# Queries' transposes ahead of the weights' fetches, and a new home for four weights, in an attention and MLP kernel

## The chip, the cores and the metric

The kernel runs on one core of a Trainium2 chip. The metric is the device time of one execution in microseconds. Its engines are named as in the profile: PE multiplies matrices (PEld loads its weights), DVE is the vector engine, ACT the scalar engine, POOL the GpSimd engine, and SP issues nearly all DMA transfers, in the order of its queue.

## What is computed

Attention over clusters, and a two-layer MLP on its result. For 4 batches and 8 heads, 768 queries and keys of 64 elements are each assigned to one of 16 clusters; a query sees only the keys of its own cluster.

```python
q_assign = argmax(q_n @ c_n.T)
k_assign = argmax(k_n @ c_n.T)
scores = scale * q @ k.T
scores = where(q_assign == k_assign, scores, -1e9)
attn = softmax(scores)
x = (attn @ v), heads joined: 3072 tokens x 512
r = maximum(x @ w_in, 0.0)
g = s * (r * r) + b
out = g @ w_out
```

w_in is 512x2048 and w_out 2048x512. All inputs and outputs are f32; the argmax and the result are computed with each f32 number as a sum of two f16 numbers, a high and a low part.

## The kernel before, in words

**Units and steps.** The attention is cut into 192 units: batch b, a third of the query rows c (256 rows), a head pair hp, one of two row tiles t, and a head h. A unit is a score product (scores, L491, into PSUM), its row maximum on DVE (maxima, L501), a bias and an exponential on ACT (exps, L508 and L511), a transposition of the result, and the product with the values. The MLP has 192 steps too: 12 blocks of 256 rows by 16 slices ft of the hidden layer. A step is a product h (mlp_in, L647), a ReLU and two squares on ACT (mlp_relu, L654 to L657), a low part on POOL (mlp_gl, L662) and the second product acc (mlp_out, L674). The main loop goes over i: unit i, the values of unit i-4, and MLP step i-21 (`LAG`).

**The first 16 units** (`RAW`) differ: the exponentials are transposed in f32 on PE (low, L535) and copied out of PSUM by DVE and ACT (L137, L135), and two units at a time are multiplied by the f32 values (values, L557, bank "m" of PSUM) and scaled on DVE (L574). After four units finish_x multiplies by the scale of the values (ACT L607), makes the high part xn (ACT L611), takes an absolute maximum (DVE L114), makes the low part (POOL L614) and transposes by DMA. After four of these, DVE L622 and a PE product find the largest x of the block, and mlp_start (L632 to L638) makes the factor that the first ReLU needs.

**Before unit 0.** prep_k and prep_q load keys and queries, scale them by a power of two, split them into high and low parts (ka, qa) and transpose these by DMA (KA, L357; QA, L411). PE multiplies KA and QA by the transposed centroids cT (pk, L366; pq, L420; cT's own transpose is L176), and onehot (L308 to L314) turns the scores into masks kb and qb, which are transposed too (KB, L370; QB, L424). A unit's scores are QA by KA plus QB by KB.

**The weights.** 32 pieces of 512 KB are fetched (fetch, through three staging buffers "stage" or gs), decoded (rebase on ACT L225; narrow on DVE L229 and L230) and bounded (bound: ACT L237 or L239, PE L242, DVE L243). The last piece lets finish_w_in and finish_w_out (DVE L264 to L279) make the two global factors; with them wsplit (ACT L287, DVE L289; 32 of each) cuts every piece into high and low parts for the MLP. The pieces and their split parts share 33 buffers of tag "w", one more than there are pieces, so each split writes into the buffer that the split before has emptied.

**What sets the order.** A scheduler places each engine's instructions by a simulated timeline and by priorities: `first_of_all` raises the priority of units under 20. `behind(x)` puts an instruction after x on the same engine's queue; it adds no wait on the hardware. The order ahead of the loop is written out at the end of the function (L740 to L768), as here:

```python
    with behind(last_turn[0], *last_split):
        some(first_v, 1)
...
        some(wgen, 4)
```

## Time and profile before

| what | value |
|---|---|
| median of three runs | 925.96 us (924.53 to 930.2) |
| the profiled execution's own time | 923.07 us |
| its span, first to last instruction | 921.4 us |
| PE busy | 829.3 us, 90% of the span |
| DVE, ACT, POOL busy | 638.4, 712.3, 545.8 us |
| mean granted clock of PE | 0.962 of full speed |

Shares of busy time are means over stages with different limits. There is a head, in which PE has little to do while keys, queries and weights are made ready; a middle, in which the first units, the splits of the weights and the first MLP steps overlap; and a long steady part with one unit and one MLP step per round. In the rows, "x" ahead of a number counts instructions, and what stands in brackets at a row's end is the idle time of that engine just before, with what ended it. The time of an execution is 1.67 us longer than its span.

### The profile page before, as it was taken

To read this page: it belongs to the slowest core of one execution; us is meant where nothing else is said; L and a number is where in the kernel's file an instruction comes from. 1 tells how busy PE (TensorE), PEld (TensorE's weight loads), DVE (VectorE), ACT (ScalarE), POOL (GpSimd) and SP (SyncE) were. 2 spreads that over 40 slices of the span, in tenths; PEclk is the share of its full clock that TensorE was granted. 3 is DMA by queue.
4 is the path that set the end of the run, shared out by engine and by line. 5 is a ranking of instruction groups with operands and counts; after the bars stand their busy time and mean duration, and the time that the engine had idled before them with its cause. 6 is when DMAs were issued, how large, how long until landed. Compare 5 with 4: busy or idle time off the path is not lost.

```text
span 921.4 us, 22828 instructions
## 1 busy us (share of the span) xinstructions
PE 829.3 (90%) x8625; PEld 589.0 (64%) x8625; DVE 638.4 (69%) x1672; ACT 712.3 (77%) x1408; POOL 545.8 (59%) x580
## 2 busy tenths in 40 slices
PE   0566877797999999999999989999999999999997
PEld 0345765564566767777667757776677777677764
DVE  7699779999676768756976567669868557563200
ACT  3479867676678879889888878988888789788553
POOL 3011127565667767777778558667776667676322
PEclk9987587998999999999999999999999999999999
DMA  6898815874786997997999888789998777666300
GB/s 174 208 276 256 223 41 104 194 155 104 172 156 143 201 189 149 170 184 143 183 181 169 182 167 164 165 166 184 177 158 169 147 133 163 121 140 142 64 24 23
DMA packets 437758, 144.23 MB, mean 157 GB/s; under 512 B 405392, under 2 KB 434064, under 8 KB 437648
## 3 DMA queue, kind: packets, MB, share of 16 engines
q1 hardware_dynamic: 437648, 142.78, 74.5%
q8 instruction: 67, 1.10, 0.5%
q14 instruction: 43, 0.35, 0.2%
HBM read 35.69 MB, written 6.29 MB: 46 GB/s over the span
## 4 chain that ended last, share of the span: by engine, by line
PE 50%; DVE 15%; DMA 8%; ACT 5%; issue 4%; POOL 2%; SPq 1%; DVEq 0%; ACTq 0%; POOLq 0%
PE h L647 18%; PE acc L674 17%; PE sc L491 7%; DMA kn<-in_k_dram 3%; DVE ssm L501 3%; DMA qn<-in_q_dram 2%; PE sc L589 2%; PE sc L591 2%; PE sc L590 2%; DVE wos L289 1%; DMA vn<-in_v_dram 1%; DVE wis L289 1%; ACT ssm L508 1%; DMA QB<-qb 1%; SPq L545 1%
## 5 line engine op out<-in xcount | busy, mean ns | idle before, releaser
L543 POOL TENSOR_TENSOR ph<-p,ph 128x768 f16<-128x768 f32 x176 | 296.8, 1687 | 148.5 <-ACT ph L135 50.0
L647 PE MATMUL h<-xk,wis 128*128 128x256 f16 x2304 | 289.1, 275 | 10.0 <-DVE wis L289 4.5
L674 PE MATMUL acc<-wos,gs 128*128 128x512 f16 x1152 | 281.7, 380 | 5.2 <-POOL gs L662 3.8
L647 PEld LDWEIGHTS <-wis 128*128 128x128 f16 x2304 | 223.0, 98 | 68.8 <-issue 7.1
L511 ACT ACTIVATE p<-sc,ssm,qsm 128x768 f32<-128x768 f32 x192 | 189.3, 986 | 4.1
L501 DVE TENSOR_REDUCE ssm<-sc 128x1 f32<-128x768 f32 x192 | 181.9, 948 | 4.1 <-PE sc L491 3.8
L662 POOL TENSOR_TENSOR gs<-r,gs 128x256 f16<-128x256 f32 x192 | 138.5, 722 | 70.6 <-ACT r L657 62.1
L674 PEld LDWEIGHTS <-gs 128*128 128x128 f16 x1152 | 104.2, 98 | 100.4 <-POOL gs L662 5.0
L508 ACT ACTIVATE ssm<-ssm,lift,qsm 128x1 f32<-128x1 f32 x192 | 73.1, 381 | 92.0 <-DVE ssm L501 90.8
L135 ACT ACTIVATE ph<-p 128x768 f16<-128x768 f32 x164 | 137.2, 837 | 0.4
L654 ACT ACTIVATE r<-h,cf 128x256 f32<-128x256 f32 x192 | 89.1, 465 | 35.5 <-PE h L647 31.1
L491 PE MATMUL sc<-KA,QA 128*128 128x384 f16 x384 | 98.6, 338 | 18.0 <-ACT p L511 13.8
L589 PE MATMUL sc<-vh,PT 128*128 128x65 f16 x1032 | 112.6, 195 | 1.1 <-DMA PT<-ph 1.1
L590 PE MATMUL sc<-vl,PT 128*128 128x64 f16 x1032 | 112.6, 192 | 0.0
L591 PE MATMUL sc<-vh,PT 128*128 128x65 f16 x1032 | 112.3, 193 | 0.0
L589 PEld LDWEIGHTS <-PT 128*128 128x128 f16 x1056 | 98.7, 97 | 12.8 <-DMA PT<-ph 1.9
L491 PE MATMUL sc<-KB,QB 128*128 128x384 f16 x384 | 99.3, 339 | 7.3 <-DMA QB<-qb 7.3
L590 PEld LDWEIGHTS <-PT 128*128 128x128 f16 x1056 | 97.9, 99 | 11.5 <-issue 0.5
L591 PEld LDWEIGHTS <-PT 128*128 128x128 f16 x1056 | 98.1, 97 | 0.0
L657 ACT ACTIVATE r<-r 128x256 f32<-128x256 f32 x192 | 79.2, 413 | 3.9
L595 DVE TENSOR_SCALAR ssm<-sc 128x1 f32<-128x1 f32 x172 | 26.3, 153 | 80.5 <-PE sc L591 79.3
L656 ACT ACTIVATE gs<-r 128x256 f16<-128x256 f32 x192 | 78.7, 411 | 1.4
(170 smaller groups left out, 1107.5 us busy)
## 6 DMA issues: line engine op xcount, KB each, us to landing
wst<-in_moe_w_in_dram SPq DMA_DIRECT2D x16, 512.0 KB, 4.7
kn<-in_k_dram SPq DMA_DIRECT2D x16, 384.0 KB, 4.0
qn<-in_q_dram SPq DMA_DIRECT2D x24, 256.0 KB, 3.6
vn<-in_v_dram SPq DMA_DIRECT2D x16, 384.0 KB, 4.0
out_dram<-o SPq DMA_DIRECT2D x12, 512.0 KB, 3.3
wst<-in_moe_w_out_dram SPq DMA_DIRECT2D x8, 512.0 KB, 4.8
gs<-in_moe_w_out_dram SPq DMA_DIRECT2D x8, 512.0 KB, 5.4
PT<-ph SPq DMA_TRANSPOSE x176, 3.5
```

Source lines behind the costliest of these rows:

```text
L135: A.activation(dst, src, AF.Copy)
L491: last_score[0] = nc.tensor.matmul(sc[:, e, :HALF], X[:, col, :], y[:, h * S + e * HALF : h * S + (e + 1) * HALF], start=st, stop=not st)
L501: last_max[0] = V.tensor_reduce(SM[i // 4][:, 0, j : j + 1], U[i]["sc"], axis=AX.XY, op=ALU.max, negate=True)
L511: last_exp[0] = A.activation(p.rearrange("p (a b) -> p a b", a=2), u["sc"], AF.Exp, bias=bi, scale=u["scale"], **total)
L543: G.tensor_tensor(u["ph"][:, 1, :], u["p"], u["ph"][:, 0, :], op=ALU.subtract)
L589: nc.tensor.matmul(o1, PT[:, kt, :], vh[:, h, kt, : D + 1], start=(kt == 0), stop=False)
L590: nc.tensor.matmul(o, PT[:, kt, :], vl[:, h, kt, :], start=False, stop=False)
L591: nc.tensor.matmul(o1, PT[:, T + kt, :], vh[:, h, kt, : D + 1], start=False, stop=(kt == T - 1))
L647: nc.tensor.matmul(ph[:, :CW], WSP[ft][0][:, wl, kt, :], XS[(b, c, kt)][:, :, xl, :], start=(i == 0), stop=(i == len(terms) - 1))
L654: A.activation(r, ph[:, :CW], AF.Relu, scale=MS[(b, c)][0])
L662: G.tensor_tensor(g[:, 1, :], r, g[:, 0, :], op=ALU.subtract)
L674: nc.tensor.matmul(acc[:, t, :], g[:, gl, rows], WSP[ft][1][:, wl, :], start=(ft == 0 and gl + wl == 0), stop=(ft == NF - 1 and gl == 1))
```

## The change

- **Order of the head.** The queries are taken one stage further ahead of the weights. The first two fetches of weights and the two scalars sv and bv now stand behind the transposes of the first queries and of the centroids (`last_qa`, `last_c`); the first piece of v, the next two fetches and the decoding of the first weight stand behind the transpose of the queries' mask and the mask itself (`last_qb`, `last_mask`).
- **Four weights live elsewhere.** Three pieces (10, 11 and 12) lie in the fifth buffer of the transposed keys, and one (31) in the fifth buffer of the split values, until they are split. So the 33 buffers of tag "w" hold 28 pieces, and five are free when the splits begin. To allow it, keys and values get fixed storage, `keys` and `halves`; batch 1's first values are split no earlier than step 36.
- **Splits from ft 4 on** stand behind xn and the absolute maximum of the fourth finish_x.
- **Values come a step earlier** (at even i for i-4, before at odd i for i-5), the fourth finish_x runs at once, and for units 8 to 15 the scale of the values is folded into the reciprocal, so that two of the four L607 go.
- **The second third's queries** (b 0, c 1) use bank "h" of PSUM for their maximum and cluster scores, not "m".

```diff
@@ -46,6 +46,7 @@
     URGENT = 20
+    SCALED = 8
 
@@ -173,7 +178,7 @@
     cT = const([P, 3, P], F16, "cT")
-    nc.sync.dma_start_transpose(cT, cnat.rearrange("p a e d -> p (a e d)"))
+    last_c = nc.sync.dma_start_transpose(cT, cnat.rearrange("p a e d -> p (a e d)"))
 
@@ -183,6 +188,20 @@
     xs_kept = const([P, 9, CT, 2, P], F16, "xk")
+
+    keys = const([P, 5, 2, 2 * T * P], F16, "keys")
+    VHW = 2 * T * (D + 2)
+    VLW = 2 * T * D
+    halves = const([P, 5, VHW + VLW], F16, "halves")
+    TW = 2 * KT * P
+    lent = {31: halves[:, 4, :TW]}
+    for j in range(3):
+        lent[10 + j] = keys[:, 4].rearrange("p e x -> p (e x)")[:, j * TW : (j + 1) * TW]
+
+    def raw_tile(p, name):
+        if p in lent:
+            return lent[p].bitcast(F32).rearrange("p (a f) -> p a f", a=KT)
+        return weight_tile(name)
 
@@ -208,10 +227,10 @@
         if p % 2 == 0:
-            w = wi[ft] = weight_tile(f"wi{ft}")
+            w = wi[ft] = raw_tile(p, f"wi{ft}")
             src = w_in.bitcast(I32)[:, ft * 2 * P : (ft + 1) * 2 * P].rearrange("(t p) f -> p t f", p=P)
         else:
-            w = wo[ft] = weight_tile(f"wo{ft}")
+            w = wo[ft] = raw_tile(p, f"wo{ft}")
             src = w_out.bitcast(I32)[ft * P : (ft + 1) * P, :].rearrange("p (a f) -> p a f", a=KT)
@@ -284,9 +303,11 @@
             e = parts(weight_tile(f"w{'io'[len(made)]}s{ft}"))
-            A.activation(e[:, 0], w, AF.Copy, scale=f)
+            with behind(*first_x[: 2 * (ft >= 4)]):
+                A.activation(e[:, 0], w, AF.Copy, scale=f)
             yield
-            V.scalar_tensor_tensor(e[:, 1], w, f, e[:, 0], op0=ALU.mult, op1=ALU.subtract)
+            with behind(*first_x[: 2 * (ft >= 4)]):
+                V.scalar_tensor_tensor(e[:, 1], w, f, e[:, 0], op0=ALU.mult, op1=ALU.subtract)
             made.append(e)
@@ -311,7 +332,7 @@
         V.tensor_tensor(o, e, m.unsqueeze(2).broadcast_to([P, nb, C]), op=ALU.is_equal)
-        eng.tensor_scalar(dst, o.unsqueeze(2).broadcast_to([P, nb, 4, C]), mul, add, op0=ALU.mult, op1=ALU.add)
+        last_mask[0] = eng.tensor_scalar(dst, o.unsqueeze(2).broadcast_to([P, nb, 4, C]), mul, add, op0=ALU.mult, op1=ALU.add)
 
@@ -351,8 +372,7 @@
         G.tensor_copy(kb[:, :, :, 0, :], ka[:, :, :, 0, :])
-        KA = sb.tile([P, 2 * T, P], F16, tag="KA", name=f"KA_{n}", bufs=5)
-        KB = sb.tile([P, 2 * T, P], F16, tag="KB", name=f"KB_{n}", bufs=5)
+        KA, KB = (keys[:, (b * NP + hp) % 5, e].rearrange("p (n q) -> p n q", q=P) for e in range(2))
         KS[(b, hp)] = (KA, KB)
@@ -387,7 +407,7 @@
             yield
-        allmax(sm[:, 1, :], qm, f"q{n}", "m" if b or c else "h")
+        allmax(sm[:, 1, :], qm, f"q{n}", "m" if b or c > 1 else "h")
         yield
@@ -408,10 +428,10 @@
         QS[(b, c, hq)] = (QA, QB, sm)
-        nc.sync.dma_start_transpose(QA, qa.rearrange("p h t e d -> p (h t e d)"))
-        yield
-        yield
-        pa = small_bank(f"pq_{n}", "m" if b or c else "h")
+        last_qa[0] = nc.sync.dma_start_transpose(QA, qa.rearrange("p h t e d -> p (h t e d)"))
+        yield
+        yield
+        pa = small_bank(f"pq_{n}", "m" if b or c > 1 else "h")
         for h in range(nh):
@@ -454,12 +474,17 @@
         V.tensor_scalar(vm[:, 7:8], vm[:, 7:8], 2.0 ** 13, None, op0=ALU.mult)
+        if b == 0:
+            V.tensor_scalar(vm[:, 4:5], vm[:, 6:7], 2.0 ** -13, None, op0=ALU.mult)
         V.tensor_scalar(vm[:, 6:7], vm[:, 6:7], 2.0 ** -19, None, op0=ALU.mult)
...
                 yield from until(RAW - 2 + 2 * hp)
-            vh = sb.tile([P, 2, T, D + 2], F16, tag="vh", name=f"vh_{b}_{hp}", bufs=5)
-            vl = sb.tile([P, 2, T, D], F16, tag="vl", name=f"vl_{b}_{hp}", bufs=5)
+            if b == 1 and hp == 0:
+                yield from until(LAG + NF - 1)
+            both = halves[:, (b * NP + hp) % 5]
+            vh = both[:, :VHW].rearrange("p (h t d) -> p h t d", h=2, t=T)
+            vl = both[:, VHW:].rearrange("p (h t d) -> p h t d", h=2, t=T)
             VS[(b, hp)] = (vh, vl)
@@ -567,7 +592,10 @@
         sums = SM[g][:, 2, j : j + 2] if i < RAW else pu[:, :, D]
-        V.tensor_scalar(rl, sums, 1e-9 * 2.0 ** 14, None, op0=ALU.add)
+        if SCALED <= i < RAW:
+            V.tensor_scalar(rl, sums, 1e-9 * 2.0 ** 14, VM[0][:, 4:5], op0=ALU.add, op1=ALU.mult)
+        else:
+            V.tensor_scalar(rl, sums, 1e-9 * 2.0 ** 14, None, op0=ALU.add)
         V.reciprocal(rl, rl)
@@ -603,13 +631,14 @@
         xs = XT.pop(g)
-        if 4 * g < RAW:
+        if 4 * g < min(SCALED, RAW):
             A.activation(xs, xs, AF.Copy, scale=VM[0][:, 7:8])
...
         xn = sb.tile([P, CT, 2, 2, D], F16, tag="xn", name=f"xn_{g}", bufs=1)
-        A.activation(xn[:, :, 0], xs, AF.Copy)
-        absmax(XM[(b, c)][:, hp : hp + 1], xs.rearrange("p t h d -> p (t h d)"))
+        made = [A.activation(xn[:, :, 0], xs, AF.Copy), absmax(XM[(b, c)][:, hp : hp + 1], xs.rearrange("p t h d -> p (t h d)"))]
+        if g == NP - 1:
+            first_x[:] = made
         yield
@@ -753,17 +782,20 @@
     some(first_k[1], 1)
+    some(first_q[0], 1)
     with behind(*last_split):
...
                 next(gen)
-    with behind(last_turn[0], *last_split):
-        some(first_v, 1)
+    with behind(last_qa[0], last_c, *last_split):
+        some(wgen, 2)
         sv = scalar_in(s_in, "sv")
         bv = scalar_in(b_in, "bv")
-        some(wgen, 4)
     run(first_k[0])
     run(first_q[0])
+    with behind(last_qb[0], last_mask[0]):
+        some(first_v, 1)
+        some(wgen, 2)
     run(first_k[1])
@@ -801,11 +833,13 @@
             mlp_gl(*steps[m - 1])
-        if i >= 5 and i % 2 == 1 and i - 5 < TURN:
+        if i >= 4 and i % 2 == 0 and i - 4 < TURN:
             with first_of_all(i):
-                values(i - 5)
-            if (i - 5) % 4 == 2:
-                active.append(finish_x((i - 5) // 4))
+                values(i - 4)
+                if i - 4 == TURN - 2:
+                    run(finish_x((i - 4) // 4))
+                elif (i - 4) % 4 == 2:
+                    active.append(finish_x((i - 4) // 4))
         background()
```

**SP's queue behind the first keys' transpose, before.** The names after the arrow tell the source: vn is v, wst and gs are staging of weights.

```order
L357 DMA_TRANSPOSE KA_1_204<-ka_170 128x12x128
L83 DMA vn_0_249<-in_v_dram 128x2x384
L141 DMA sv<-in_moe_s_dram 128x1
L141 DMA bv<-in_moe_b_dram 128x1
L83 DMA wst_256<-in_moe_w_in_dram 128x4x256
L176 DMA_TRANSPOSE cT<-cnat 128x3x128
L83 DMA wst_259<-in_moe_w_out_dram 128x1024
L83 DMA wst_262<-in_moe_w_in_dram 128x4x256
L83 DMA gs<-in_moe_w_out_dram 128x1024
L411 DMA_TRANSPOSE QA_0_0_199<-qa_0_0_185 128x8x128
L370 DMA_TRANSPOSE KB_0_194<-kb 128x12x128
L424 DMA_TRANSPOSE QB_0_0_200<-qb_0_0_186 128x8x128
```

The same place with the change:

```order
L377 DMA_TRANSPOSE keys<-ka_172 128x12x128
L181 DMA_TRANSPOSE cT<-cnat 128x3x128
L431 DMA_TRANSPOSE QA_0_0_199<-qa_0_0_187 128x8x128
L88 DMA wst_247<-in_moe_w_in_dram 128x4x256
L88 DMA wst_250<-in_moe_w_out_dram 128x1024
L146 DMA sv<-in_moe_s_dram 128x1
L146 DMA bv<-in_moe_b_dram 128x1
L390 DMA_TRANSPOSE keys<-kb 128x12x128
L444 DMA_TRANSPOSE QB_0_0_200<-qb_0_0_188 128x8x128
L88 DMA vn_0_319<-in_v_dram 128x2x384
L88 DMA wst_322<-in_moe_w_in_dram 128x4x256
L88 DMA gs<-in_moe_w_out_dram 128x1024
```

cT moves up past v, the scalars and one weight, QA past v, the scalars and four weights, KB and QB past v and two weights.

**DVE from the first keys' mask to the queries' mask, before** (oo and oe are steps of onehot, kb and qb the masks, wi and wo weights in decoding):

```order
L314 TENSOR_SCALAR kb<-oo_k_0_296 128x12x64
L230 SCALAR_TENSOR_TENSOR wi_261<-wst_262,wi_261 128x512
L229 TENSOR_SCALAR wo_267<-wo_267 128x512
L230 SCALAR_TENSOR_TENSOR wo_267<-gs,wo_267 128x512
L308 TENSOR_REDUCE om_q_0_0_321<-pq_0_0_304 128x8
L309 TENSOR_TENSOR oe_q_0_0_322<-pq_0_0_304,om_q_0_0_321 128x128
L311 TENSOR_TENSOR oe_q_0_0_322<-oe_q_0_0_322,rev 128x128
L312 TENSOR_REDUCE om_q_0_0_321<-oe_q_0_0_322 128x8
L313 TENSOR_TENSOR oo_q_0_0_323<-oe_q_0_0_322,om_q_0_0_321 128x128
L308 TENSOR_REDUCE om_k_1_356<-pk_1_331 128x12
L314 TENSOR_SCALAR qb_0_0_186<-oo_q_0_0_323 128x8x64
```

With the change, L248 and L249 are the old L229 and L230, and L329 to L335 the old L308 to L314:

```order
L335 TENSOR_SCALAR kb<-oo_k_0_283 128x12x64
L329 TENSOR_REDUCE om_q_0_0_308<-pq_0_0_291 128x8
L330 TENSOR_TENSOR oe_q_0_0_309<-pq_0_0_291,om_q_0_0_308 128x128
L332 TENSOR_TENSOR oe_q_0_0_309<-oe_q_0_0_309,rev 128x128
L333 TENSOR_REDUCE om_q_0_0_308<-oe_q_0_0_309 128x8
L334 TENSOR_TENSOR oo_q_0_0_310<-oe_q_0_0_309,om_q_0_0_308 128x128
L329 TENSOR_REDUCE om_k_1_354<-pk_1_329 128x12
L335 TENSOR_SCALAR qb_0_0_188<-oo_q_0_0_310 128x8x64
L248 TENSOR_SCALAR wi_246<-wi_246 128x512
L248 TENSOR_SCALAR wo_249<-wo_249 128x512
L330 TENSOR_TENSOR oe_k_1_355<-pk_1_329,om_k_1_354 128x192
L249 SCALAR_TENSOR_TENSOR wi_246<-wst_247,wi_246 128x512
```

Four weights' decoding stood among the masks of keys and queries; now none stands ahead of the queries' mask qb, and two follow it.

**ACT from the fourth high part xn to the first ReLU, before** (wis and wos are split parts):

```order
L287 ACTIVATE wis_1524<-wi_480,glob 128x512
L611 ACTIVATE xn_1448<-xs_1366 128x2x128
L287 ACTIVATE wos_1594<-wo_488,glob 128x512
L511 ACTIVATE p_1419<-sc_1410,ssm_1313,qsm_1_0_822 128x768
L508 ACTIVATE ssm_1480<-ssm_1480,lift,qsm_1_0_822 128x1
L287 ACTIVATE wis_1596<-wi_548,glob 128x512
L654 ACTIVATE r_0_0_1579<-h_0_0_1566,cf_0_1562 128x256
L287 ACTIVATE wos_1653<-wo_556,glob 128x512
L656 ACTIVATE gs<-r_0_0_1579 128x256
L657 ACTIVATE r_0_0_1579<-r_0_0_1579 128x256
```

With the change (L307 is the old L287, L639 the old L611, L536 and L533 the old L511 and L508, L683 the old L654), the beginning of it:

```order
L639 ACTIVATE xn_1397<-xs_1332 128x2x128
L307 ACTIVATE wis_1577<-wi_542,glob 128x512
L307 ACTIVATE wos_1634<-wo_550,glob 128x512
L307 ACTIVATE wis_1640<-keys,glob 128x512
L307 ACTIVATE wos_1700<-keys,glob 128x512
L307 ACTIVATE wis_1705<-keys,glob 128x512
L307 ACTIVATE wos_1781<-wo_684,glob 128x512
L307 ACTIVATE wis_1785<-wi_722,glob 128x512
L536 ACTIVATE p_1428<-sc_1419,ssm_1303,qsm_1_0_819 128x768
L533 ACTIVATE ssm_1469<-ssm_1469,lift,qsm_1_0_819 128x1
L307 ACTIVATE wos_1863<-wo_730,glob 128x512
L307 ACTIVATE wis_1865<-wi_790,glob 128x512
```

Ahead of the first ReLU stood two splits after xn; now fifteen stand there, these nine and six more, with three exponentials, two biases and one copy ph among them.

## Rows read from the trace of the kernel before

**Rows 1.** Busy time of each engine in stretches of the span (window: length, then busy us and instructions of PE, PEld, DVE, ACT and POOL; then PE's granted clock, the DMA engines' share and GB/s).

```profile
0.00:36.00 36.00, 6.24 (x82) 3.90 (x83) 27.82 (x91) 14.53 (x26) 10.58 (x42) 1.00 0.67 179
36.00:120.00 84.00, 62.78 (x437) 48.27 (x435) 71.26 (x172) 66.22 (x144) 9.90 (x12) 0.76 0.86 235
145.00:260.00 115.00, 97.85 (x998) 65.42 (x998) 101.34 (x224) 83.95 (x161) 72.41 (x66) 0.94 0.72 149
260.00:866.00 606.00, 593.26 (x6643) 423.59 (x6641) 413.17 (x1122) 508.49 (x997) 430.48 (x433) 1.00 0.83 162
```

**Rows 2.** SP's queue in the order of time: start, length, what is issued.

```profile
15.26 0.59 SPq L83 DMA_DIRECT2D vn<-in_v_dram  x1
...
17.54 1.19 SPq L176 DMA_TRANSPOSE cT<-cnat  x1
...
22.19 1.43 SPq L411 DMA_TRANSPOSE QA<-qa  x1
...
32.84 1.23 SPq L424 DMA_TRANSPOSE QB<-qb  x1
...
41.11 1.25 SPq L86 DMA_DIRECT2D wst<-in_moe_w_in_dram  x1
```

**Rows 3.** What PE waited for up to 140 us (total us, times, longest), and, from the view of transfers between 10 and 45 us, how many of a kind were issued and the median us from issue to landing.

```profile
PE pk L366 <- DMA cT<-cnat: 6.2, 1, 6.2
...
PE sc L491 <- DMA QA<-qa: 4.1, 1, 4.1
...
KA<-ka SPq DMA_TRANSPOSE x4, 3.6
...
cT<-cnat SPq DMA_TRANSPOSE x1, 6.3
...
QB<-qb SPq DMA_TRANSPOSE x1, 2.8
```

**Rows 4.** POOL's copy that completes qa, and DVE from the last keys' split to the first row maximum, in the order of time.

```profile
19.05 0.61 POOL L407 COPY qa<-qb 128x512 f16<-128x512 f16 x1
...
21.85 1.01 DVE L206 SCALAR_TENSOR_TENSOR ka<-kn,ksm,ka 128x768 f16<-128x768 f32 x1
...
24.66 0.36 DVE L308 TENSOR_REDUCE om_k<-pk 128x12 f32<-128x192 f32 x1 [1.53 <-PE pk L367]
...
32.49 0.28 DVE L314 TENSOR_SCALAR qb<-oo_q 128x512 f16<-128x512 f16 x1
...
34.40 0.36 DVE L314 TENSOR_SCALAR xk<-oo_k 128x768 f16<-128x768 f16 x1
...
36.52 1.82 DVE L501 TENSOR_REDUCE ssm<-sc 128x1 f32<-128x768 f32 x2 [1.77 <-PE sc L491]
```

**Rows 5.** Stretches as in Rows 1, shorter.

```profile
36.00:46.60 10.60, 7.96 (x61) 5.45 (x59) 5.66 (x9) 5.25 (x12) 0.00 (x0) 1.00 1.11 240
...
60.00:80.00 20.00, 15.01 (x110) 11.64 (x110) 18.31 (x50) 15.13 (x33) 2.45 (x3) 0.66 0.95 278
...
118.90:138.80 19.90, 15.89 (x109) 13.07 (x109) 14.99 (x42) 12.19 (x22) 5.47 (x5) 0.83 0.21 48
138.80:181.50 42.70, 33.62 (x338) 22.69 (x334) 39.76 (x84) 30.89 (x61) 27.26 (x23) 0.88 0.72 151
181.50:225.00 43.50, 34.49 (x356) 22.68 (x357) 42.74 (x92) 33.33 (x64) 29.50 (x27) 0.91 0.61 128
```

**Rows 6.** DVE's groups between 36.5 and 119 us by line and shape (count, busy us, mean ns of one, idle time before them).

```profile
L230 DVE SCALAR_TENSOR_TENSOR wi<-wst,wi 128x512 uint32<-128x512 uint32 x14 | 10.0, 713 | 0.0
...
L229 DVE TENSOR_SCALAR wo<-wo 128x512 int32<-128x512 int32 x14 | 6.1, 432 | 2.1 <-ACT wo L225 2.0
```

**Rows 7.** From the bound of the last weight to the first ReLU: five instructions of DVE and PE, and one of ACT, each with its start and length.

```profile
118.94 0.16 DVE L273 TENSOR_REDUCE amb_w<-l 128x1 bf16<-128x16 f32 x1
...
135.72 0.29 DVE L574 TENSOR_TENSOR xs<-px,ssm 128x128 f32<-128x128 f32 x1 [0.22 <-PE px L557]
...
138.37 0.42 DVE L114 TENSOR_REDUCE xm<-xs 128x1 f32<-128x256 f32 x1 [1.32 <-ACT xs L607]
138.82 0.16 DVE L622 TENSOR_REDUCE amb_x<-xm 128x1 bf16<-128x4 f32 x1
...
124.65 4.91 PE L557 MATMUL px<-vn,PT 128*128 128x64 f32 x24 [1.24 <-DVE qsm L111]
...
144.76 0.46 ACT L654 ACTIVATE r<-h,cf 128x256 f32<-128x256 f32 x1
```

**Rows 8.** The splits: one alone on DVE, one beside POOL's L543, one on ACT; an exponential's group between 36.5 and 119 us; all of DVE's splits between 138.8 and 225 us (window: length, then their busy us and count, PE's granted clock, the DMA engines' share and GB/s); and the row maxima of the steady part with their first and last start.

```profile
124.52 0.74 DVE L289 SCALAR_TENSOR_TENSOR wis<-wi,glob,wis 128x512 f16<-128x512 f32 x1
...
179.03 1.64 POOL L543 TENSOR_TENSOR ph<-p,ph 128x768 f16<-128x768 f32 x1 [1.51 <-issue]
179.04 2.17 DVE L289 SCALAR_TENSOR_TENSOR wos<-wo,glob,wos 128x512 f16<-128x512 f32 x1
...
145.68 0.72 ACT L287 ACTIVATE wos<-wo,glob 128x512 f16<-128x512 f32 x1 [0.46 <-DVE wis L289]
...
L511 ACT ACTIVATE p<-sc,ssm,qsm 128x768 f32<-128x768 f32 x16 | 15.7, 980 | 0.2
...
138.80:225.00 86.20, 29.77 (x26) 0.90 0.66 140
...
L501 DVE TENSOR_REDUCE ssm<-sc x149: 940/947/958, 260.8 to 853.6; 128x1 f32<-128x768 f32 x149
```

More of the change, by code (lines that the diff above doesn't have):

```diff
@@ L74, in tile_cluster_attention_mlp @@
     last_transpose = [None]
+    first_x = [None, None]
     last_turn = [None]
+    last_qa = [None]
+    last_qb = [None]
+    last_mask = [None]
     last_split = [None, None]
@@ L113, in absmax @@
     def absmax(dst, src, axis=AX.X):
-        V.tensor_reduce(dst, src, axis=axis, op=ALU.max, apply_absolute_value=True)
+        return V.tensor_reduce(dst, src, axis=axis, op=ALU.max, apply_absolute_value=True)
     rev = const([P, C], F32, "rev")
@@ L423, in prep_q @@
         yield from onehot(pa, nh * CT, f"q{n}", mk, BIG, 0.0, G if b or c or hq else V)
-        nc.sync.dma_start_transpose(QB, qb.rearrange("p h t e d -> p (h t e d)"))
+        last_qb[0] = nc.sync.dma_start_transpose(QB, qb.rearrange("p h t e d -> p (h t e d)"))
     VS = {}
```

## Prediction

> **What bounds the kernel now.** I read the stretches first. From 260 to 866 us PE is busy 593.26 of 606 us, at full granted clock [rows 1]: 98%, with nothing to win there, and the change leaves that work as it is. The 149 row maxima of this part start between 260.8 and 853.6 us [rows 8], so a unit and an MLP step take 592.8 / 148 = 4.005 us. Before it PE is not the bound: 6.24 of 36 us, then 62.78 of 84, then 97.85 of 115 [rows 1]. There the reader is to ask what PE waits for. The view of waits names the centroids' transpose, 6.2 us, and the queries', 4.1 us [rows 3]; SP's queue [rows 2] shows why: cT is issued at 17.54 behind v, the scalars and a weight, QA at 22.19 behind three more weights, though the copy that completes qa ended at 19.66 [rows 4]. DVE then is busy 18.31 of 20 us while weights are decoded, 14.99 of 19.90 between the last weight's bound and x's maximum, and 39.76 of 42.70 and 42.74 of 43.50 in the stretches to units 27 and 36 [rows 5]. So up to 225 us the bound is mostly DVE, with holes in which a chain of waits runs, and an end that comes earlier by d makes the whole earlier by d if nothing takes it back before 260 us.
>
> The sum is made against the profiled execution, 923.07 us; the median of the runs is 925.96, so I subtract the sum from the median.
>
> **Term 1, the head.** QA can go once qa is ready, near 19.7 instead of 22.19. cT stands where v was issued, 15.26, and lands in 3.6 (like KA) to 6.3 us (as it did) [rows 2, 3], at 18.9 to 21.6, ahead of 22.9, when DVE ends its last keys' split and can take the keys' mask; before, that waited until 24.66 [rows 4]. In before's sequence four decodings of 0.43 + 0.71 us [rows 6], 4.6 us less their overlap, stood between that start and the end of qb at 32.77 [rows 4]. Without them the two masks take some 8.1 - 4.1 = 4 us: qb is ready near 27 us if QA has landed by 23.3 (3.6 after issue), near 29.6 if QA takes the 6.5 us that passed between its issue and PE's go before (22.19 to 28.72: the wait of 4.1 us ends there). QB is then issued at 27.3, between 26.9 and 29.8, not at 32.84. The first row maximum stood 36.52 - 32.84 = 3.7 us behind QB's issue [rows 2, 4]: now 31.0 (30.6 to 33.5), **5.5 us earlier**, 3.0 to 5.9.
>
> But decoding that was done in that time is only moved. Behind the first maximum DVE now has two more weights, one bound and one mask: 2 x 1.14 us, and some 0.9 for a bound and for the part of a mask that slips behind, 3.2 us. From 36 to 46.6 us DVE had 10.60 - 5.66 = 4.9 us idle [rows 5], where these may go, but fetches also have to come: their stream went on at 41.11 [rows 2], behind the second keys' transposes, whose mask (it ended at 34.76 [rows 4]) now follows the first maximum: 31.0 + 0.95 + 0.36 = 32.3, 2.4 us earlier. Both bounds say that the last weight's bound (118.94, rows 7's first) moves by at least 2.3 us, and at most by the 5.5. I take **-3.5**: nearer the fetches, since ACT and DVE of the decoding stand behind them.
>
> v, the scalars and the first weights land later. v is first used by a maximum that is not urgent, the scalars at the end of the decoding: nothing.
>
> **Term 2, from the last weight to x's maximum**, 118.94 to 138.82, 19.9 us with 14.99 of DVE [rows 5, 7], floor 4.9 below. Here the px product waited 1.24 us for the bank that the queries' maximum held, and the last of the first 16 units' values is followed by ACT's L607: DVE's L574 ended at 136.0 and the next maximum began at 138.37, 1.32 us of it waiting for L607 [rows 7]. The bank wait goes, L607's 0.5 us and the wait go: 1.24 + 2.3 = 3.5. Values a step earlier take PE work out of the stretch, too; two splits come into it. I take **-3.5**, from 0 (another wait takes the place: PE's own order) to -4.4 (the floor with those splits in it, less other waits).
>
> **Term 3, the splits.** Five free buffers let ACT run ahead of DVE: fifteen splits stand ahead of the first ReLU. At one per 0.63 us (0.72 less the overlap with the next), three exponentials of some 0.9, two biases and a copy, that is 13.4 us from xn, where 144.76 - 138.82 = 5.9 were needed [rows 7, 8]. So the MLP begins up to 7.5 us later relative to xn. DVE is the bound there: by the orders it has some 6.3 us more work done by unit 27's maximum, twelve splits more less MLP and other work, and by unit 36 it is level again (0.4 us). From unit 27 to 36 before took 43.5 us and PE's pace would allow 9 x 4.005 = 36.0, so 7.5 us can be given back. PE's order has the same steps between units, thus what the MLP is late by is not lost at the end. I take **-0.5**, between -4 (splits less blocked) and +5 (a late MLP leaves PE short).
>
> A split is 0.74 us alone, and 2.17 beside POOL's L543 of 1.64 us, which began 0.01 us ahead of it [rows 8]; 26 of them took 29.77 us, 1.145 each, so (1.145 - 0.74) / 1.43 = 28% of them paid such a block. The Trainium skill, page "SBUF — State Buffer", section "Who interferes with whom", says that a vector instruction with two SBUF inputs contends with a GpSimd instruction that reads SBUF, and that the one that comes second fully blocks. By that rule the trace agrees, and it speaks against packing splits closer: if all 24 splits behind xn met an L543 it would cost, by the rows' 2.17, an estimated 24 x (2.17 - 1.145) = 25 us, and the sum would be +17; by the 28% of the rows it stays as below.
>
> The rest has one answer: fixed storage for keys and values and the split of batch 1's first values held to step 36 lie where PE is the bound, at nothing; if that cover fails, the wait is for values due at unit 48, some 12 steps or 48 us later.
>
> **Sum**: -3.5 - 3.5 - 0.5 = -7.5, so 915.6 on the profiled execution's scale and **918.5** as a median. The bounds of the likeliest case, not all at once, make 914 to 922.
>
> **The rivals.**
> - A, the holes close (0.20): the 3.2 us vanish in DVE's idle time, term 1 keeps 5.5, term 2 reaches its floor of 4.9, the splits lose a tenth of a us each on 24. -5.5 - 4.9 - 2.4 = -12.8: 913. For it: DVE idle 4.9 of 10.6 us. Against: 18.31 of 20 us busy later.
> - B, fetches bound the head (0.16): term 1 gives 2.3 and the bank's wait is followed by another: 925.96 - 2.3 = 923.7. For it: a DMA share of 1.11 and 0.95 in the stretches of decoding [rows 5]. Against: DVE is busy 92% at the same time.
> - C, the other side: the splits block (0.10). In the stretch to unit 27 POOL's L543 is dense and DVE is the bound, so each longer split is on the path. If two thirds rather than 28% of 24 splits wait for an L543, each takes 0.74 + 0.67 x 1.43 = 1.69, 24 x 0.55 = 13 us more: -7.5 + 13 = +5.5, 931.5. It decides the sign from a mean of 1.145 + 7.5 / 24 = 1.46 us, half of them blocked. Against: with the MLP late, POOL's other work is late too.
> - D, it does not do what it says (0.04): order on a queue is no wait, and data that is not there earlier leaves all as it was, 926.
>
> The forecast has 0.50.
>
> **How the numbers follow.** A measurement of this kernel tells about 1% from no change, so faster is below 916.7 and slower above 935.2. Of the forecast's own range two fifths lie below, 0.20; with A's 0.20 that is 0.40. Same: 0.30 of the forecast, B, D, and the lower half of C (0.05) make 0.55. Slower 0.05, the other half of C. The range goes from A with the outer bounds of terms 1 and 3, -5.9 - 4.9 - 4 = -14.8, less the 1.4 us that the fastest run lies below the median, 909.7, so 909, to 926 (B and D); it leaves out C and the tails.
>
> **What would show it.** Term 1: QA issued near 19.7, QB near 27.3, first maximum near 31, the last weight's bound near 115.4; a row maximum at 31 with the bound at 117 or later speaks for B. Term 2: 16.4 us from there to x's maximum, with no wait for L607 and none of px for the queries' bank. Term 3: the first ReLU near 145, unit 36's maximum near 217, and from there the same pace of 4.005 us. The mean of the splits behind xn tells C: 1.46 or above. I would be wrong if the pace of the steady part changes, which no term touches, or if the fetches' stream, not DVE, sets the end of decoding.

## The result and the profile after

| | before | changed |
|---|---|---|
| median (range), 4 runs each | 928.08 us (924.53 to 930.21) | 911.94 us (909.31 to 913.72) |
| the profiled execution, its span | 923.07, 921.4 us | 912.4, 910.7 us |

The ratio is 0.9844, 95% interval 0.9813 to 0.9874: faster by 1.3 to 1.9%. A second comparison, among the experiments, gave 0.9877 (0.9831 to 0.9923). The two profiled executions are 10.7 us apart; they are what the traces explain. In one batch of before's runs the two shortest, 916.88 and 918.69 us, show a mean granted clock of 0.970 and 0.972, the two longest, 927.71 and 928.71 us, one of 0.954 and 0.955.

First SP's queue of the changed kernel:

```profile
17.00 1.18 SPq L181 DMA_TRANSPOSE cT<-cnat  x1
19.15 1.23 SPq L431 DMA_TRANSPOSE QA<-qa  x1
...
27.25 1.24 SPq L444 DMA_TRANSPOSE QB<-qb  x1
28.54 0.57 SPq L88 DMA_DIRECT2D vn<-in_v_dram  x1
29.16 0.46 SPq L88 DMA_DIRECT2D wst<-in_moe_w_in_dram  x1
29.67 0.50 SPq L88 DMA_DIRECT2D gs<-in_moe_w_out_dram  x1
32.17 1.44 SPq L390 DMA_TRANSPOSE keys<-xk  x1
33.71 5.27 SPq L377 DMA_TRANSPOSE keys<-ka  x2
...
40.42 0.53 SPq L91 DMA_DIRECT2D wst<-in_moe_w_in_dram  x1
```

QA and QB go 3.0 and 5.6 us earlier than in [rows 2]. But the stream of weights, last row, goes on only 0.7 us earlier: two keys' transposes ahead of it take 5.27 us, behind a piece of v and two weights that now go out between 28.5 and 30.2. Before, the same two took 3.31 us:

```profile
36.31 3.31 SPq L357 DMA_TRANSPOSE KA<-ka  x2
```

In the nine profiled executions here that have the new order of the head and two fetches in that place, they take 4.81 to 5.27 us, in the four with the old order 3.30 to 3.37.

DVE in the changed kernel: first row maximum, the last weight's bound, x's maximum, unit 36's row maximum, and the 149 maxima of the steady part:

```profile
30.91 0.96 DVE L526 TENSOR_REDUCE ssm<-sc 128x1 f32<-128x768 f32 x1 [0.55 <-PE sc L516]
...
118.37 0.16 DVE L292 TENSOR_REDUCE amb_w<-l 128x1 bf16<-128x16 f32 x1
...
134.28 0.16 DVE L651 TENSOR_REDUCE amb_x<-xm 128x1 bf16<-128x4 f32 x1
...
220.51 0.95 DVE L526 TENSOR_REDUCE ssm<-sc 128x1 f32<-128x768 f32 x1
...
L526 DVE TENSOR_REDUCE ssm<-sc x149: 939/947/950, 252.3 to 843.0; 128x1 f32<-128x768 f32 x149
```

Read against [rows 4, 7, 8], the lead is 5.6 us at the first maximum, 0.6 at the last weight's bound, 4.5 at x's maximum, 4.5 at unit 36 (225.01 before), 8.5 where the steady part begins and 10.6 where it ends. So more than half of it appears behind unit 36. One trace is one execution: in a second profiled execution of the changed kernel (span 907.6 us, among the experiments) the leads are 4.8, 2.1, 6.7, 6.5, 10.6 and 13.7 us. Its last weight's bound and its steady part:

```profile
116.87 0.16 DVE L292 TENSOR_REDUCE amb_w<-l 128x1 bf16<-128x16 f32 x1
...
L526 DVE TENSOR_REDUCE ssm<-sc x149: 940/947/951, 250.2 to 839.9; 128x1 f32<-128x768 f32 x149
```

So a milestone of one trace, and PE's work below, tell nothing finer than some 2 us between two kernels. The stretches say what it is made of, first of the changed kernel, then of before (columns as in Rows 1):

```profile
0.00:36.00 36.00, 9.55 (x92) 5.58 (x93) 29.10 (x92) 14.88 (x27) 10.89 (x41) 1.00 0.71 188
36.00:120.00 84.00, 62.62 (x434) 50.31 (x434) 71.24 (x174) 66.90 (x145) 9.46 (x12) 0.74 0.86 233
120.00:180.00 60.00, 45.07 (x377) 32.40 (x378) 56.76 (x121) 43.88 (x82) 25.97 (x24) 0.77 0.48 104
180.00:285.00 105.00, 101.09 (x1127) 69.48 (x1124) 79.71 (x216) 80.90 (x157) 76.87 (x76) 1.00 0.87 167
285.00:910.70 625.70, 611.94 (x6601) 434.13 (x6599) 394.37 (x1074) 506.14 (x1000) 420.83 (x429) 1.00 0.77 150
```

```profile
120.00:180.00 60.00, 48.37 (x439) 35.26 (x437) 52.19 (x118) 41.79 (x78) 30.68 (x26) 0.86 0.55 116
180.00:285.00 105.00, 90.35 (x946) 60.46 (x944) 85.13 (x197) 76.03 (x145) 69.57 (x69) 0.95 0.73 149
285.00:921.40 636.40, 621.59 (x6728) 441.13 (x6728) 401.99 (x1098) 513.75 (x1015) 425.10 (x433) 1.00 0.77 150
```

PE's idle time, length less busy, changes from 29.8 to 26.5 us up to 36 us, hardly up to 120, from 11.6 to 14.9 up to 180, from **14.7 to 3.9** between 180 and 285, and from 14.8 to 13.8 behind. These are -3.3, +0.2, +3.3, -10.7 and -1.0, -11.6 in all; PE's own busy time grew by 0.9. Behind 180 PE has the full granted clock and hardly a hole. There is no split left there: ACT's last one begins at 175.85, where before 222.73 was the last. The longest hole of before between 180 and 285 us did wait for a split, just ahead of unit 36:

```profile
222.75 2.31 PE L647 MATMUL h<-xk,wis 128*128 128x256 f16 x10 [4.04 <-DVE wis L289]
```

That makes 4.0 of the 10.7 us of idle time that went there; the other holes of before in this stretch are of 1.8 us and less and waited for other things, so the end of the splits is not shown to be what closed those (a kernel below has splits up to 215 us and hardly more holes). ACT of the changed kernel, xn, three splits, the first ReLU, the last split:

```profile
134.01 0.40 ACT L639 ACTIVATE xn<-xs 128x256 f16<-128x256 f32 x1
...
138.66 0.72 ACT L307 ACTIVATE wos<-wo,glob 128x512 f16<-128x512 f32 x1 [1.18 <-DVE wis L310]
...
140.90 0.72 ACT L307 ACTIVATE wis<-wi,glob 128x512 f16<-128x512 f32 x1 [1.52 <-DVE wos L310]
...
145.46 0.72 ACT L307 ACTIVATE wos<-wo,glob 128x512 f16<-128x512 f32 x1 [2.39 <-DVE wos L310]
...
155.62 0.82 ACT L683 ACTIVATE r<-h,cf 128x256 f32<-128x256 f32 x2
...
175.85 0.72 ACT L307 ACTIVATE wos<-halves,glob 128x512 f16<-128x512 f32 x1 [0.96 <-DVE wos L310]
```

After five splits in a row, up to 137.5, ACT waits for DVE to free a buffer, six times and for 7.2 us in all up to the first ReLU, and the first ReLU, behind them in the queue, comes 10.9 us later than in [rows 7].

### The profile page after: what moved, and what is told of

Same layout as the page of the kernel before. It is cut to its first block, busy times and chain, and to the rows that moved or that the text cites. A ratio compares the mean times of both kernels' runs of the same rounds, so it can differ in the third digit from the quotient of the medians.

```text
span 910.7 us, 22840 instructions
## 1 busy us (share of the span) xinstructions
PE 830.3 (91%) x8625; PEld 591.9 (65%) x8625; DVE 631.2 (69%) x1673; ACT 712.7 (78%) x1406; POOL 544.0 (60%) x580
## 4 chain that ended last, share of the span: by engine, by line
PE 44%; DVE 21%; DMA 14%; ACT 9%; issue 6%; POOL 3%; SPq 2%; DVEq 0%; ACTq 0%; POOLq 0%
PE h L676 15%; PE acc L703 14%; PE sc L516 7%; DMA kn<-in_k_dram 4%; DVE ssm L526 4%; DMA qn<-in_q_dram 4%; ACT p L536 2%; PE sc L617 2%; PE sc L619 2%; ACT ssm L533 2%; PE sc L618 2%; DMA vn<-in_v_dram 2%; DVE ka L225 2%; SPq L570 1%; POOL ph L568 1%
## 5 line engine op out<-in xcount | busy, mean ns | idle before, releaser
L536 ACT ACTIVATE p<-sc,ssm,qsm 128x768 f32<-128x768 f32 x192 | 189.3, 986 | 4.3
L691 POOL TENSOR_TENSOR gs<-r,gs 128x256 f16<-128x256 f32 x192 | 136.1, 710 | 64.3 <-ACT r L686 55.3
L533 ACT ACTIVATE ssm<-ssm,lift,qsm 128x1 f32<-128x1 f32 x192 | 73.0, 381 | 83.2 <-DVE ssm L526 82.5
L683 ACT ACTIVATE r<-h,cf 128x256 f32<-128x256 f32 x192 | 89.1, 465 | 39.8 <-PE h L676 34.0
L617 PE MATMUL sc<-halves,PT 128*128 128x65 f16 x1032 | 113.0, 195 | 0.1
L618 PE MATMUL sc<-halves,PT 128*128 128x64 f16 x1032 | 112.9, 192 | 0.0
L619 PE MATMUL sc<-halves,PT 128*128 128x65 f16 x1032 | 112.6, 193 | 0.0
L516 PE MATMUL sc<-keys,QA 128*128 128x384 f16 x384 | 99.8, 341 | 12.8 <-ACT p L536 10.9
L516 PE MATMUL sc<-keys,QB 128*128 128x384 f16 x384 | 99.7, 341 | 8.3 <-DMA QB<-qb 8.3
L618 PEld LDWEIGHTS <-PT 128*128 128x128 f16 x1056 | 98.1, 99 | 11.6 <-issue 0.7
```

Source lines behind the costliest of these rows:

```text
L516: last_score[0] = nc.tensor.matmul(sc[:, e, :HALF], X[:, col, :], y[:, h * S + e * HALF : h * S + (e + 1) * HALF], start=st, stop=not st)
L533: A.activation(bi, sm[:, 0, j : j + 1], AF.Identity, scale=u["scale"], bias=lift)
L536: last_exp[0] = A.activation(p.rearrange("p (a b) -> p a b", a=2), u["sc"], AF.Exp, bias=bi, scale=u["scale"], **total)
L617: nc.tensor.matmul(o1, PT[:, kt, :], vh[:, h, kt, : D + 1], start=(kt == 0), stop=False)
L618: nc.tensor.matmul(o, PT[:, kt, :], vl[:, h, kt, :], start=False, stop=False)
L619: nc.tensor.matmul(o1, PT[:, T + kt, :], vh[:, h, kt, : D + 1], start=False, stop=(kt == T - 1))
```

## The experiments

Two numbers serve most of them: **PE work left at 285 us** (PE's busy time from there to the end, at full clock; before 621.6, changed 611.9), which tells the lead gained by then (the second execution of the changed kernel has 609.7, so 2 us are noise), and **PE's idle time behind 285 us** (14.8 and 13.8). The order of instructions in the steady part isn't touched by any edit, but the scheduler makes it anew for each kernel.

**One part alone.** Each of three kernels keeps one part of the change and takes the two others back, by these edits:

```diff
 the order of the head taken back
-    some(first_q[0], 1)
-    with behind(last_qa[0], last_c, *last_split):
-        some(wgen, 2)
+    with behind(last_turn[0], *last_split):
+        some(first_v, 1)
...
+        some(wgen, 4)
...
-    with behind(last_qb[0], last_mask[0]):
-        some(first_v, 1)
-        some(wgen, 2)
 the homes and the splits' place taken back
-    lent = {31: halves[:, 4, :TW]}
...
+    lent = {}
...
-            with behind(*first_x[: 2 * (ft >= 4)]):
+            with behind():
...
-                yield from until(LAG + NF - 1)
 the values taken back
-    SCALED = 8
+    SCALED = 16
...
-"m" if b or c > 1 else "h"
+"m" if b or c else "h"
...
-                values(i - 4)
...
+                values(i - 5)
```

> Only the new order of the head (the queries' and centroids' transposes ahead of the weights), the rest as before. Theory (the stream of weights sets the end of decoding, and it goes on only 0.7 us earlier): the first row maximum 5.6 us earlier, near 31, the last weight's bound within 1.5 us of before's 118.9, the time within 2 us of before, say -1. Rival (the earlier queries carry through): the last bound near 114, the time -4 to -6.

Measured 1.0033 (1.0008 to 1.0059): no gain. First maximum at 32.0, last bound at 124.27, later than the theory and the rival had it, and yet x's maximum 2.1 us earlier than before (136.71); work left 620.2, idle behind 285 us 18.9.

> Only the other homes of four weights and the splits from ft 4 on behind the fourth xn; order of the head and values as before. Theory (the splits end before unit 27 and PE is then busy without holes up to unit 48): x's maximum about as before (138.8), first ReLU some 8 us later than before, unit 48's row maximum 4 us earlier than before, the time -5 (-3 to -7). Rival (the gain comes from the values' chain, and the splits only shift work): the time within 2 us of before.

1.0134 (1.0087 to 1.0181), slower: neither had that. First ReLU 143.4, but the second at 158.9; splits over at 182; PE idle between 180 and 285 7.3 us, half of before's. Yet work left was 623.6 and idle behind 285 us 23.2.

> Only the values one step earlier, the scale folded for units 8 to 15, the fourth finish_x at once, and the other bank for the second third's queries. Theory: x's maximum 4 us earlier than before, near 135, and the time -4 at most, for DVE is the bound up to unit 36 and may eat part of it: -1 to -4. Rival (all of the gain hangs on this chain): -8 or more.

0.998 (0.9952 to 1.0009), not to be told from no change. x's maximum came at 134.93, as the theory had it; work left 621.8: by 285 us the lead was gone.

**One part taken away from the changed kernel.**

> The changed kernel with the old order of the head. Theory: the first row maximum back at 36.5, but the last weight's bound within 1.5 us of the changed kernel's 118.4, and the time within 2 us of the changed kernel's. Rival (the head carries through): 4 to 6 us slower than the changed kernel.

0.9949 (0.9925 to 0.9974), 0.7 to 1% slower than the changed kernel, so my theory fell on the time, though the last bound (116.99) and x's maximum (134.69) stand as they were. Work left 619.7: 7.8 us of lead are gone by 285 us. They go late: unit 29's maximum is 1.0 us behind the changed kernel's, unit 30's 5.1 (198.97 for 193.90), and ahead of unit 30's scores PE waits for a later queries' transpose:

```profile
191.54 0.20 PE L440 MATMUL pq<-cT,QA 128*128 128x16 f16 x1 [3.10 <-DMA QA<-qa]
```

In the changed kernel this wait is 1.38 us long, so it makes 1.7 of the 4.1 us. That the early queries of the head carry the gain is therefore not shown; the order around unit 30 changed with them.

> The changed kernel with its four weights back in the common buffers (one spare) and the splits free to stand ahead of the fourth xn: head and values as changed. Theory (up to 225 us DVE with the splits is the bound, so what head and values win is eaten there): row maxima of units 0 and 16 and x's maximum as in the changed kernel within 2 us, splits until 215 to 225 us, PE idle 180 to 285 us about 14 us instead of 3.9, time within 4 us of before, 7 to 14 slower than the changed kernel. Rival (head and values carry by themselves): -8 or more against before.

0.9985 (0.9957 to 1.0014). The time is the theory's, but not the reason. x's maximum came at 129.04, 5.2 us earlier than in the changed kernel. The splits lasted to 215, yet PE idle between 180 and 285 was 5.9 us, and work left 613.3, nearly the changed kernel's: an early end of the splits isn't needed for that. The gain was lost behind 285 us, where idle time was 23.8.

> The changed kernel with the values at odd steps, all four L607, the fourth finish_x among the rest, and the old bank of the second queries; head and homes as changed. Theory: x's maximum 4 us later than in the changed kernel (near 138), first ReLU later by as much, splits over by 185, PE idle 180 to 285 us 4 to 8 us, time 4 to 6 us slower than the changed kernel. Rival (homes with a late MLP are a loss, as alone): 10 or more slower than the changed kernel, before's time or above.

1.0015 (0.9989 to 1.004), 13 to 16 us slower than the changed kernel, as the rival had it; but x's maximum, at 137.85, and PE's idle time between 180 and 285 us, 5.6, were the theory's, and work left was 612.4. Idle behind 285 us was 21.8. Again the loss lies where no part of the change stands. The stretch 335 to 435 us (columns as in Rows 1), of the kernels without homes, without values, and of the changed one:

```profile
335.00:435.00 100.00, 93.01 (x1044) 65.66 (x1042) 68.64 (x196) 78.63 (x155) 66.92 (x68) 0.98 0.78 148
```

```profile
335.00:435.00 100.00, 93.30 (x1061) 66.03 (x1058) 67.26 (x195) 80.28 (x158) 68.45 (x69) 1.00 0.80 157
```

```profile
335.00:435.00 100.00, 99.58 (x1132) 71.36 (x1131) 72.16 (x205) 87.95 (x172) 75.01 (x76) 1.00 0.87 168
```

Seven us of PE are lost in 100, on both. Of PE's nearly 17000 rows in the built programs the last 12936, from unit 53 on, stand in one order in before, the changed kernel and the one without the head; of head alone, homes alone, no homes and no values only the last 7062, from unit 120 on, agree with the changed kernel's. What such an order does is seen in the kernel with the values alone (11326 rows agree), SP's queue and PE:

```profile
361.95 1.40 SPq L375 DMA_TRANSPOSE keys<-ka  x1
363.40 1.31 SPq L429 DMA_TRANSPOSE QA<-qa  x1
...
368.50 0.18 PE L438 MATMUL pq<-cT,QA 128*128 128x16 f16 x1 [2.39 <-DMA QA<-qa]
```

In before's order QA stood ahead of the keys there, and was issued at 359.67; here it is second, and PE stands still for 2.39 us ahead of its cluster scores.

**The splits' place.** Only `behind(*first_x ...)` is taken out of both lines of wsplit.

> The changed kernel without the order that puts splits from ft 4 on behind the fourth xn and its maximum. Theory: five spare buffers then let splits stand ahead of x's maximum, which comes 3 to 6 us later, and the time is 2 to 5 us slower than the changed kernel. Rival (ACT and DVE have holes there for them): x's maximum within 1.5 us, the time the same or up to 3 us faster, since the splits end sooner.

0.9857 (0.9819 to 0.9896). x's maximum did come 3.9 us later, 138.2, as the theory had it, but the splits were over at 168 (179 with the order), and work left was 607.5: the theory's time fell. Beside the changed kernel on one chip:

> The changed kernel once more, as the measure for the three beside it, and as the second half of its comparison with before: 12 to 16 us faster than before.

0.9877 (0.9831 to 0.9923), 912.29 us, 11.4 us below before's median there, a little less than expected.

> The kernel without the order that puts splits behind the fourth xn, beside the changed kernel on the same chip. If the PE work left at 285 us tells it (607.5 against 611.9): 3 to 5 us faster than the changed kernel. Rival (its fast profile was chance): within 1 us.

0.9867 (0.9813 to 0.9921), 910.33 us: 2.0 us less, not to be told from the changed kernel; work left was 608.0 against 609.7. That part of the change does nothing that these runs could tell.

**What sets the last weight's bound.** A fifth staging buffer takes the place where pieces 11 and 12 lived:

```diff
-    for j in range(3):
-        lent[10 + j] = keys[:, 4].rearrange("p e x -> p (e x)")[:, j * TW : (j + 1) * TW]
+    spare = keys[:, 4].rearrange("p e x -> p (e x)")
+    lent[10] = spare[:, 2 * TW : 3 * TW]
+    st5 = spare[:, : 2 * TW].bitcast(I32).rearrange("p (a f w) -> p a f w", a=KT, w=2)
...
-        if p % 4 == 3:
+        if p % 5 == 4:
+            st = st5
+        elif p % 5 == 3:
```

> The changed kernel with a fifth staging buffer for the weights' fetches, in the place where three of the four weights lived until split (one of the three stays; two go back to the common buffers, so three of these are free at the splits, not five). Theory (a fetch waits until a piece four before it is decoded, some 9.8 us a round, and this loop sets the decoding's 78 us): the last weight's bound 6 to 10 us earlier than 118.4, DVE's idle time from 36 us to it down to a few us, the time 3 to 8 us less than the changed kernel's. Rival (the engines' order sets it, not the buffers): the last bound within 2 us of 118.4 and the time the same or slower, as two spare buffers are gone.

0.9917 (0.9891 to 0.9944), 916.05 us, 3.8 us slower than the changed kernel beside it, though their runs overlap (911.51 to 919.29 and 909.37 to 914.76). DVE of this kernel, the last weight's decoding and the last bound:

```profile
105.69 0.69 DVE L252 SCALAR_TENSOR_TENSOR halves<-wst,halves 128x512 uint32<-128x512 uint32 x1
...
117.75 0.16 DVE L295 TENSOR_REDUCE amb_w<-l 128x1 bf16<-128x16 f32 x1
```

The decoding ended 9.8 us earlier than in the changed kernel (115.53), so the buffers did limit it; but the bound came as in the changed kernel (118.37), as the rival had it. The last pieces' bounds stand in DVE's queue among the units' work, where DVE waited for PE's pw and sc by turns, and units 8 to 16 took 48.2 us, hardly less than in the changed kernel (49.6, and 47.9 in its second execution).

The next kernel has this buffer, and behind the queries' mask `some(wgen, 4)` for `some(wgen, 2)`.

> As the run before, and weights 4 and 5 fetched ahead of the third and fourth keys' transposes, where the first fetches stand. Theory (the stream's standstill from 30 to 40 us costs the decoding two weights): the last bound another 3 to 5 us earlier than with the fifth buffer alone. Rival (the keys' transposes, now later, hold units 8 to 15): no earlier, and unit 12's maximum 3 us or more later.

0.9815 (0.9772 to 0.9859), 906.41 us, its four runs (904.4 to 908.75) all below the four of the changed kernel beside it (909.37 to 914.76): the fastest version here. SP's queue, then DVE at unit 8 and at the last bound:

```profile
30.46 0.43 SPq L88 DMA_DIRECT2D keys<-in_moe_w_in_dram  x1
31.00 0.64 SPq L88 DMA_DIRECT2D wst<-in_moe_w_out_dram  x1
37.04 2.33 SPq L393 DMA_TRANSPOSE keys<-xk  x1
```

```profile
61.54 0.96 DVE L529 TENSOR_REDUCE ssm<-sc 128x1 f32<-128x768 f32 x1
...
108.46 0.15 DVE L295 TENSOR_REDUCE amb_w<-l 128x1 bf16<-128x16 f32 x1
```

With weights 4 and 5 fetched in the gap, unit 8 stands 6.5 us earlier than with the fifth buffer alone, and the last bound 9.3 us, more than the theory expected. The keys' transposes went out later (37.04 for 33.03), and the maxima of units 3 to 5 came 1.3 to 3.0 us later, but none behind them. This agrees with the theory that the stream's standstill is where the head's lead went, but it doesn't show it by itself: the decoding ended no earlier (its last step began at 106.66, for 105.69), and the order changed too, for between 31 us and unit 8 DVE decodes nine weights here and twelve with the fifth buffer alone. How much of the 9.3 us is the fetches and how much the order is open.

**Is it the order?** The kernel without homes gets one idle DVE maximum, which the scheduler places at the start of DVE's queue (2.90 us), where DVE waits for data:

```diff
+        if i == 22:
+            with tc.high_priority(offset=300):
+                V.tensor_reduce(idle, ident, axis=AX.X, op=ALU.max)
```

> The kernel without the four homes and without the splits' order, plus one idle DVE maximum over a 128x128 constant (0.28 us) that stands at the very start of DVE's queue, where DVE waits for data. It changes only what the scheduler makes of the rest: the last 14474 of 16737 rows of PE's order are now those of the changed kernel, where they were 7062 without the idle instruction. Theory (the steady part's order, not the homes, cost that kernel its gain: PE idle behind 285 us 23.8 against 13.8): PE idle behind 285 us 11 to 16 us, PE work left there about as in the changed kernel (613 before), time 7 to 11 less than without the idle instruction, 911 to 916, or a ratio of 0.988 to 0.992 to before. Rival (the holes come from the missing homes or from the runs themselves): within 3 us of the kernel without it, a ratio of 0.996 to 1.001.

```profile
335.00:435.00 100.00, 99.09 (x1088) 70.06 (x1087) 69.17 (x200) 86.24 (x168) 72.14 (x71) 1.00 0.92 165
```

The holes went, 7.0 us idle became 0.9, with the homes still missing: in this stretch the order was the cause. Idle behind 285 us fell from 23.8 to 17.4, not to the 11 to 16 of the theory; the other holes stayed. The time was 1.003 (1.0007 to 1.0054), no better but rather worse, and outside what the theory and the rival said: the idle instruction turned the order ahead of 285 us too, and work left was 622.4, 9 us more. So an instruction of 0.28 us moves PE's work left by as much as a part of the change does.

## Why the prediction was right or wrong

The direction and the range held; 918.5 forecast was too slow by 6.6 us, the time lies below the bounds of the likeliest case (914 to 922), and the gain, 7.5 us, was about half of the medians' 16.1 and two thirds of the 11.4 of the second comparison. A time below 916.7, which came, had a chance of 0.40, one not to be told from no change 0.55. By its terms, with the second profiled execution in brackets:

- **Term 1, the first maximum: right.** QA at 19.15 (19.7 forecast), QB at 27.25 (27.3), first maximum at 30.91 (31.0). Only cT was issued at 17.00 and not near 15.26, but it landed in 2.3 us, within the time that the forecast allowed.
- **Term 1, the last weight's bound: mis-sized**, -0.6 (-2.1) for -3.5, outside its bounds of -2.3 to -5.5, in the second execution by little. The failing step was "2.4 us earlier" for the stream of fetches: the mask did end 2.6 us earlier (its transpose issued at 32.17 for 34.78), but I let the keys' transposes take what they took before, 3.31 us. They took 5.27, behind the transfers that the change had put ahead of them, and the stream went on 0.7 us earlier. Rival B had the place right and asked for 2.3 still. The step behind it is weak too: with a fifth buffer the decoding ended 9.8 us earlier and the bound 0.6, so the bound doesn't simply follow the decoding; the units' work in DVE's queue counts as well.
- **Term 2: right in size**, -4.0 (-4.7) for -3.5: 118.37 to 134.28 is 15.9 us, 16.4 forecast. DVE's idle time in the stretch fell from 4.9 to 1.2 us, and the wait for L607 is gone. But the waits of the px products, 1.24 us before, did not go: they are 0.74 and 1.16 now, for other work of DVE. And the 2.3 us put down to L607 held a split of 0.75 us, which stands elsewhere now. That the values move x's maximum is shown by two kernels: alone they bring it 3.9 us earlier, taken away it comes 3.6 us later.
- **Term 3: right by its number, not by its course.** Up to unit 36 it was 0 (a lead of 4.5 there as at x's maximum; 6.5 for 6.7), -0.5 forecast. But the first ReLU came at 155.62 and not near 145, 21.6 us behind xn for 13.4, because ACT waited 7.2 us for DVE's splits, which the 13.4 left out.
- **The main miss: nothing was put behind unit 36**, where I took PE to be the bound. It was not, before. Another 4.0 us (4.1) came in from unit 36 to unit 43, where the steady part starts (8.5 less 4.5). These two stretches, before and changed (columns as in Rows 1), say what they are:

```profile
225.01:260.85 35.84, 34.07 (x347) 22.93 (x345) 25.76 (x69) 23.90 (x46) 20.30 (x22) 0.96 0.77 156
```

```profile
220.51:252.34 31.83, 31.45 (x333) 21.15 (x334) 23.50 (x64) 22.82 (x42) 21.77 (x22) 1.00 0.91 176
```

  1.4 us are PE's idle time (1.8 for 0.4) and 2.6 its busy time. Of these 1.3 are 11 more h products (83 for 72): in the built order one MLP step's stand ahead of unit 36 in the changed kernel and behind it before, so that "the same steps between units" did not hold, and this much had been won earlier. The other 1.3 go with the granted clock, 0.96 for 1.00: a score product took 353 ns on the mean, for 326.
- **The steady part's pace**, the forecast's own sign of being wrong, changed: 590.7 / 148 = 3.991 us (3.984) for 4.005, which makes 2.1 us (3.1). Part of it is idle time, 13.8 us (12.9) behind 285 us for 14.8; what the rest is, is open.
- **Rival C fell.** The splits were blocked less, not more (the window of all splits behind xn, columns as in Rows 8):

```profile
134.30:180.00 45.70, 23.34 (x24) 0.78 0.59 128
```

  0.97 us each for 1.145. POOL was busy 22.42 us in this window, for 25.76 in the same window of before, which fits the argument against C; nothing tests it. **Rival A** named an end near the truth, 913, and its term 2 came near, but the rest by other ways: DVE was as busy from 36 to 120 us as before, 71.24 for 71.26, so no hole closed there. **D** fell.
- **"The rest has one answer": half wrong.** For this change PE's order from unit 53 on stayed, by luck of the scheduler. In four of the partial kernels it did not, and PE's idle time behind 285 us was 5 to 10 us longer.

The leads from milestone to milestone are -0.6, -4.0, 0.0, -4.0 and -2.1, 10.7 us (-2.1, -4.7, +0.2, -4.1 and -3.1, 13.8); they add up by construction, and only what is said of each tells why. Why the medians lie 11 to 16 us apart and the profiles 10.7 stays open: before's runs spread over 917 to 930 us, its profiled one being at 923.07. Open too, and not shown by any run, is how much belongs to which part. Alone the parts gave +0.3, +1.3 and -0.2%, together -1.6 and -1.2%, and each taken away cost 0.7 to 1.7%; since the order of the whole changes with each, these are not the parts' own prices.

## What to carry to other kernels

Follow a lead from milestone to milestone (first maximum, last bound, x's maximum, unit 36, the steady part's ends) and with PE's work left at a fixed time: here an early lead of 5.6 us was lost within 90 us but for 0.6 (2.1), and more than half of the gain showed behind unit 36, where the forecast had no term. A milestone on one engine can stand at another place in the work of a second one; count that engine's instructions between two milestones before you call the difference idle time. When a transfer is put into another's place, ask what goes out behind it, and let that take longer. Where a scheduler makes the order, compare the built order of the stretches that an edit does not touch before giving their time to the edit, and try an idle instruction as a control. Profile the same kernel twice: two executions differed by 2 us at the milestones here.

## What was not expected of the hardware

Two transposes of keys issued together took 3.31 us of SP's queue before, where the DMA engines' share of the 4.3 us ahead had been 0.35, and 5.27 us behind 1.4 MB of fetches (384 KB of v, two weights of 512 KB) issued some 4 us before, with a share of 0.96 in the 5.2 us ahead. One more staging buffer let the decoding end 9.8 us earlier, and the kernel was not faster. Two executions of the changed kernel had a granted clock of 0.74 and 0.80 from 36 to 120 us, and the second was 2 us ahead at x's maximum; what set the clocks apart no run here shows.
